# Eight identity products ahead of the feed-forward part's first transpositions, and other settings of the order there and in the start

## The chip, the core and the metric

The kernel runs on one core of a Trainium2 chip. Time is the device time of one execution in microseconds (us). A core has a matrix engine (TensorE, PE in the profile, with its weight loads as PEld), a vector engine (DVE), a scalar engine (ACT), a general engine (POOL) and a sync engine (SP) that here issues nearly all transfers between the main memory and the core. Each engine takes its instructions strictly in the order in which the program lists them, and waits on semaphores where an operand comes from another engine.

## What is computed

One transformer block on 2048 rows of 512 numbers, in 32-bit floats: a conditioned normalization, windowed attention (32 heads of 16, each row sees itself and the 255 rows before it), a second conditioned normalization and a gated feed-forward part of width 1792.

```python
mod = (_silu(c) @ w_mod).reshape(c.shape[0], 6, 1, -1)
sa, ca, ga, sb, cb, gb = (mod[:, i] for i in range(6))
h = _layernorm(x) * (1 + ca) + sa
x = x + ga * _A_ref(h, A_wqkv, A_wo)              # softmax(q k^T / 4, window 256) v, then wo
h = _layernorm(x) * (1 + cb) + sb
x = x + gb * _B_ref(h, B_w1, B_w3, B_w2)          # (silu(h w1) * (h w3)) w2
```

## The kernel before

Matrix products are made from two parts of each operand (a rounded high part and the rest), three products for each full one. The work has four stretches.

**The start.** The rows are loaded in 16 tiles of 128, the six modulation vectors are computed (`modulation`), the rows are normalized, transposed and split (`ln1`, in four blocks of 512 rows; `ring_fill` clears buffers of the scores on POOL), the values of all 16 tiles are computed (`values`, PE line L653), and the first steps of the attention's units are done: `unit_a` (queries and keys, PE L438, with `rows` copying them into place) for three units, `unit_b` (row maxima: a PE product L485 per half, a maximum on DVE L494 each, then `parts` on DVE, `turn` on PE L509, `cut` on ACT and `rows` on SP) for two. Everything here has a key: `W` gives the times of the groups, `Y` the offsets inside `unit_a` and `unit_b`. The list sorted by these keys is the order of the program, and with it that of each engine.

**The units.** 32 units of attention follow (8 groups of four heads times 4 blocks of 512 rows). Step u runs `unit_a` for one unit, `unit_b` for one that is further and `unit_c` for u itself (scores L753, masks by DVE or POOL, exponentials on ACT, products with the values L721), by the keys in `X`, which the change leaves alone.

**The change-over.** Units whose key is at or above TS = 229.9 go into a second list, `fixed`, at times from the map `us` (constants `TW`), and a planner (`Sched.deal`) deals all remaining operations of the program between and behind them: the denominators of the attention (`o_sums`: a load, a reciprocal on DVE L1072, a store), their products with the outputs and the split into two parts (`o_part`: loads L1087 and L1092, DVE or POOL L1104, ACT L1096, DVE or POOL L1099), the output projection (`o_proj`, PE L1116) with the sums of the second normalization behind it (`add_stats`, DVE L985, ACT L993), that normalization (`ln_rstd`, `ln2`: ACT L1236, transpositions on PE L1250, ACT L1254, sums on DVE or POOL L1267, parts L1273 and L1275), and the loads and splits of weights (`load_w`, `load_w2`: SP L1174 and L1217, ACT L967, POOL L968). The planner starts an operation at the earliest time at which its operands are there by its own estimates; among those that are ready on an engine the lowest key wins. Keys come from `K`. Three constants widen the estimates: `RATE` and `QUIET` (transfers), `PEM` (added to the time at which an operand from ACT, DVE or POOL is there for PE) and `DM` (added to the time at which a transfer is there for an engine that uses it, for operations before the end of the `fixed` list). `K["by"][b][k]` names the engines of `o_part` (product, difference); `K["be"]` those of the splits in `load_b`.

**The feed-forward part.** Two halves of 1024 rows, seven pairs of column blocks each: products L1378 (`ffn`), gate and up combined on ACT, DVE and POOL, products L1471 with the second weight, sums into the rows, stores. Its order is dealt by the same planner.

Of the kernel before, what the change touches and what calls it, by code (L numbers as in the profile page):

```python
# [18 lines left out]
P = 128  # L19
# [20 lines left out]
         10.575, 10.975, 11.087, 6.249, 6.261), o=(11.83, 12.324), job=(0.275, 3.004, 9.681), gate=7.93)  # L40
Y = dict(wqk=(-1.668, 4.008, 4.272), pj=(0.205, 0.587, 0.969, 1.18, 1.719, 2.115, 2.497, 2.879, 3.261,
         3.583, 3.954, 4.423), ev=(4.619, 4.869), mix=(5.37,), row=(4.926, 4.905, 4.873, 5.915, 5.14, 5.105,
         6.405, 6.405, 6.405), mx=(0.022, 0.523, 1.023, 1.523, 2.023, 2.822, 3.023, 3.33, 4.051, 4.523, 5.023,
         5.249, 6.023, 6.523, 7.023, 7.523), tl=(0.092, 0.371, 0.331, 0.34, 0.405, 0.331, 0.331, 0.331, 0.331,
         0.331, 0.331, 0.331, 0.331, 0.119, 0.331, 0.331), mr=(8.465, 8.547, 8.884, 10.016))
MODE = 'CDCPCDCP'
W = dict(m=0.18, s=0.307, a=0.29, t=0.562, p=0.366, vs=1.748, vo=0.433, wq=(-1.444, 1.47, 1.587), wv0=-2.239, wvh=(-0.578, -0.445, -0.399, -0.345), wvl=(-0.193, -0.326, -0.374, -0.317), wp=1, A0=2.112, h0=0.452, h=6.002, hb=6.868, ls=3.035, la=0.875, rf=(-1.1, -0.393, 6.445), v=2, vt=1.562, mr=(-1.837, 1.507), mm=(3.653, 5.841, 7.356, 7.655), ml=(-1.346, 1.651, 2.536, 6.904), A=1.465, At=7.897, B=10.563)
MXB = 3
STB = 3
MODL = 'CECECECE'  # L50
NL = 3
XB = 6
PTB = 9
# [202 lines left out]
INF = float("inf")  # L256
RATE = 320.0

QUIET = 1.487
KEY = 1.715  # L260
# [3 lines left out]
def us(t):  # L264
# [3 lines left out]

TW = (231.0, 241.0, 0.8, 0.583)

# [19 lines left out]

@with_exitstack
def block_kernel(ctx: ExitStack, tc: tile.TileContext, x, wqk, wv, wo, w13, w2, c, wmod, out):
    nc = tc.nc
# [4 lines left out]
    ident = cst.tile([P, P], F32, name="ident")  # L298
# [87 lines left out]
    for hh in range(2):  # L386
        m = mskq[HP * hh:HP * hh + HP]
# [213 lines left out]
    wvh = p0.tile([P, KC, D], F32R, name="wvh")  # L601
    wvl = p0.tile([P, KC, D], F32R, name="wvl")
# [69 lines left out]
    h0 = -40.0  # L672
# [17 lines left out]
    for b in range(1, NB):  # L690
        h = h0 + W["h"] + W["hb"] * (b - 1)
# [532 lines left out]
    def ln2(half, key):  # L1224
# [17 lines left out]
        def rows_k(k, key):  # L1242
            h = {}
            for n, (kk, t) in enumerate(((k, 0), (k + 2, 1), (k, 1), (k + 2, 0))):
                bk = Bank("up")
                hk, hn = (half, k, kk, t), f"t{n}"

                def turn(kk=kk, t=t, bk=bk):
                    for i in range(4):
                        nc.tensor.transpose(ps(bk)[:, i * P:(i + 1) * P],  # L1250
                                            tiles["xn", half, 4 * t + i][:, kk * P:(kk + 1) * P], ident)
# [354 lines left out]
```

## Time and profile before

| | us |
|---|---|
| median of three runs | 954.08 (952.42 to 954.97) |
| the profiled execution, its own time | 952.06 |
| its span, from the first instruction to the last | 950.3 |
| PE busy in it | 916.3 |
| DVE, ACT, POOL busy | 670.0, 525.1, 545.6 |

Everything below is read from one execution. Its time is 1.76 us more than its span, which lies outside the first and the last instruction, and 2.02 us under the median. A row of the timeline has the start, the length, the engine, the line, the operation with output and input, the count, and in brackets for how long the engine had been idle and what ended that. A row of the windows has, for each engine, the busy time in a stretch and the number of instructions, then the mean clock that PE was granted (1.00 is full), the busy share of the transfer engines and their GB/s.

### The profile page before, as it was taken

To read this page: it belongs to the slowest core of one execution; us is meant where nothing else is said; L and a number is where in the kernel's file an instruction comes from. 1 tells how busy PE (TensorE), PEld (TensorE's weight loads), DVE (VectorE), ACT (ScalarE), POOL (GpSimd) and SP (SyncE) were. 2 spreads that over 40 slices of the span, in tenths; PEclk is the share of its full clock that TensorE was granted. 3 is DMA by queue.
4 is the path that set the end of the run, shared out by engine and by line. 5 is a ranking of instruction groups with operands and counts; after the bars stand their busy time and mean duration, and the time that the engine had idled before them with its cause. 6 is when DMAs were issued, how large, how long until landed. Compare 5 with 4: busy or idle time off the path is not lost.

```text
span 950.3 us, 16719 instructions
## 1 busy us (share of the span) xinstructions
PE 916.3 (96%) x5330; PEld 710.3 (75%) x5330; DVE 670.0 (71%) x1861; ACT 525.1 (55%) x1031; POOL 545.6 (57%) x694
## 2 busy tenths in 40 slices
PE   5999999999999999988987999999999999999998
PEld 3688677777777777755765878888888888888886
DVE  7675789888898989876668565665558645566465
ACT  3333777777777777766577754333455334433330
POOL 6220566676757566645566789977659546453420
PEclk9999899999999999988989999999999999999999
DMA  8621465555655555565960659645244512323002
GB/s 296 200 80 46 113 185 163 158 146 164 183 156 150 170 157 147 136 183 167 298 220 12 221 199 322 222 171 166 90 161 157 187 41 99 99 62 97 26 23 89
DMA packets 125020, 141.62 MB, mean 149 GB/s; under 512 B 60034, under 2 KB 72834, under 8 KB 124932
## 3 DMA queue, kind: packets, MB, share of 16 engines
q1 hardware_dynamic: 124212, 139.51, 48.0%
q10 hardware_dynamic: 720, 1.05, 0.3%
q8 instruction: 42, 0.69, 0.3%
q14 instruction: 46, 0.38, 0.1%
HBM read 85.72 MB, written 34.61 MB: 127 GB/s over the span
## 4 chain that ended last, share of the span: by engine, by line
PE 78%; DVE 6%; DMA 4%; POOL 4%; ACT 3%; issue 2%; SPq 2%; POOLq 0%; DVEq 0%; ACTq 0%
PE st L1378 11%; PE mx L1378 10%; PE pj L438 8%; PE st L753 8%; PE mx L485 8%; PE po L721 8%; PE st L1471 7%; PE mx L1471 7%; PE st L653 5%; PE pj L1378 3%; PE pj L1471 2%; DMA r_dr<-mT 1%; DVE t L1267 1%; DVE b L1275 1%; DMA qk<-o_dr 1%
## 5 line engine op out<-in xcount | busy, mean ns | idle before, releaser
L494 DVE CUSTOM_DVE_ANT_0 junk<-mx,mskq 128x320 bf16<-128x320 f32 (+4 forms) x512 | 223.4, 464 | 39.6 <-PE mx L485 39.0
L968 POOL TENSOR_TENSOR w<-w,w 128x512 fp32r<-128x512 f32 (+2 forms) x56 | 107.0, 1924 | 111.6 <-ACT w L967 61.8
L485 PE MATMUL mx<-ringk,ringq 96*128 96x320 f32 (+4 forms) x512 | 154.9, 326 | 2.2 <-DVE mt L494 2.2
L753 PE MATMUL st<-ringq,ringk 98*128 98x256 f32 (+1 forms) x528 | 141.9, 338 | 6.8 <-DVE st L773 2.5
L780 POOL TENSOR_SCALAR_AFFINE_SELECT pt<-pt 128x256 f32<-128x256 f32 x224 | 92.4, 413 | 74.7 <-ACT pt L768 67.0
L438 PE MATMUL pj<-hT,wq 128*128 128x512 f32 x384 | 132.5, 403 | 0.3 <-DVE wq L427 0.3
L485 PEld LDWEIGHTS mx<-ringk,ringq 96*128 96x128 f32 x512 | 98.6, 193 | 41.4 <-DVE mt L494 23.1
L768 ACT ACTIVATE pt<-st 128x512 f32<-128x512 f32 (+1 forms) x198 | 115.2, 587 | 24.7 <-DVE st L773 10.5
L753 PEld LDWEIGHTS st<-ringq,ringk 98*128 98x128 f32 x528 | 91.8, 194 | 22.2 <-ACT pt L768 5.8
L721 PE MATMUL po<-pt,vS 128*17 128x384 f32 (+2 forms) x1408 | 92.7, 394 | 0.0
L438 PEld LDWEIGHTS pj<-hT,wq 128*128 128x128 f32 x384 | 68.4, 192 | 7.8 <-DVE wq L427 0.8
L1378 PE MATMUL st<-b,w 128*128 128x512 f32 x270 | 67.8, 391 | 1.3 <-ACT t L1412 1.3
L1409 DVE TENSOR_TENSOR t<-st,t 128x512 f32<-128x512 f32 x48 | 33.0, 688 | 43.3 <-PE st L1378 28.5
L1409 DVE TENSOR_TENSOR t<-mx,t 128x512 f32<-128x512 f32 x49 | 33.5, 687 | 41.8 <-PE mx L1378 28.0
L721 PEld LDWEIGHTS po<-pt,vS 128*17 128x17 f32 x1408 | 34.6, 98 | 36.3 <-issue 19.8
L1449 ACT ACTIVATE wq<-g 128x512 fp32r<-128x512 f32 x28 | 17.7, 631 | 77.2 <-DVE g L1405 38.1
L1378 PE MATMUL mx<-b,w 128*128 128x512 f32 x240 | 59.9, 389 | 0.0
L773 DVE COPY_PREDICATED st<-later,st 128x256 f32<-128x256 uint8 x112 | 47.5, 424 | 17.3 <-PE st L753 12.7
L1378 PEld LDWEIGHTS st<-b,w 128*128 128x128 f32 x270 | 50.5, 188 | 12.1 <-ACT t L1412 1.7
L795 POOL TENSOR_SCALAR_AFFINE_SELECT sm<-sm 128x256 f32<-128x256 f32 x109 | 42.3, 406 | 29.5 <-ACT sm L785 28.6
L761 DVE TENSOR_TENSOR st<-st,mskr 128x256 f32<-128x256 f32 x125 | 53.6, 429 | 8.0 <-PE st L753 8.0
L967 ACT ACTIVATE w<-w 128x512 fp32r<-128x512 f32 (+2 forms) x56 | 42.5, 786 | 20.7 <-DMA w<-wsum 11.2
(256 smaller groups left out, 2010.6 us busy)
## 6 DMA issues: line engine op xcount, KB each, us to landing
ringq<-qk SPq DMA_DIRECT2D x192, 64.0 KB
ringk<-qk SPq DMA_DIRECT2D x96, 128.0 KB
o_dr<-os SPq DMA_DIRECT2D x32, 256.0 KB
w<-wsum SPq DMA_DIRECT2D x14, 512.0 KB
w<-w2g SPq DMA_DIRECT2D x14, 512.0 KB
jb<-in_w SPq DMA_DIRECT2D x24, 256.0 KB
wraw<-in_w SPq DMA_DIRECT2D x7, 768.0 KB
w<-wraw SPq DMA_DIRECT2D x14, 384.0 KB
```

What stands on the lines that cost most here:

```text
L438: nc.tensor.matmul(v["ps"], WQ[g][w][:, n // 3], hTp(i, n // 3, b * BT, BT), start=(n == 0), stop=(n == 3 * KC - 1))
L485: nc.tensor.matmul(v[i][:, :n], both_queries(a, gs), keys(NS, a, (gs + 1) * HP - n, n), start=True, stop=True)
L494: nc.vector.tensor_tensor_reduce(out=junk[:, :n], in0=v[i][:, :n], in1=mskq[:, WK - n:], scale=1.0, scalar=-3e38, op0=ALU.add, op1=ALU.max ...
L721: nc.tensor.matmul(po[32 * i:32 * i + DH + 1, qb * P:(qb + nq) * P], vS[:, kb, 4 * g + i], pts[i // 2][:, i % 2, c0:c0 + nq], start=first, ...
L753: nc.tensor.matmul(o, keys(NM, a, kb * P, P), queries(a, q, n), start=q == lo, stop=not plus and q + n == hi, skip_group_check=True)
L761: nc.vector.tensor_tensor(out=ps, in0=ps, in1=mskk[:, p:p + 1].to_broadcast([P, 2, P]), op=ALU.add)
L768: nc.scalar.activation(held[u, j, a][:, :, :n], v[j, a, 0].rearrange("p (h q) k -> p h q k", h=2)[:, :, :n], AF.Exp, scale=SCALE)
L780: nc.gpsimd.affine_select(out=pt[:, :, 2 * m], in_=pt[:, :, 0], **w)
L968: sch.op(eng, lambda: on_eng(eng).tensor_tensor(out=lo(), in0=src(), in1=hi().bitcast(F32), op=ALU.subtract), 0.06 + 0.0024 * n if eng == ...
L1378: nc.tensor.matmul(ps(bk), WT[s, n][w][:, col], BB[t, k][r], start=start and c == 0, stop=stop and c == 5, skip_group_check=True)
L1409: return nc.vector.tensor_add(o, x, y)
L1471: nc.tensor.matmul(ps(bk), tiles[hk + (h,)][:, i * P:(i + 1) * P], w2_of(last, y, f), start=(m == 0), stop=(m == 5))
```

## The change

Two lines of code are new, and all else is settings.

- `warm` issues `WARM` = 8 products of the 128x128 identity with itself into a bank, each overwriting the last. The first of the `turn` steps of `ln2` (half 0, k = 0, n = 0) calls it on its own bank, ahead of its four transpositions, which then overwrite it too.
- `Y` and `W`: other keys in the start. `ring_fill` for blocks 1 and 2 now sorts ahead of the first normalization on POOL, three of its steps; the load of the first query and key weight sorts behind a modulation load and two row loads on SP; the transposition at the end of `unit_b` and some of its maxima sort later.
- `RATE`, `QUIET`, `TW`, `PEM` and `DM`: other constants of the planner's estimates.
- `K`: other keys in the change-over and in the feed-forward part, and other engines for some operations of `o_part` (23 of 32 on DVE where 19 were) and one of `load_b`.

```diff
-Y = dict(wqk=(-1.668, 4.008, 4.272), pj=(0.205, 0.587, 0.969, 1.18, 1.719, 2.115, 2.497, 2.879, 3.261,
...
-         5.249, 6.023, 6.523, 7.023, 7.523), tl=(0.092, 0.371, 0.331, 0.34, 0.405, 0.331, 0.331, 0.331, 0.331,
-         0.331, 0.331, 0.331, 0.331, 0.119, 0.331, 0.331), mr=(8.465, 8.547, 8.884, 10.016))
+Y = dict(wqk=(-2.274, 2.035, 4.308), pj=(-0.1, 0.569, 1.019, 1.185, 1.631, 2.138, 2.581, 2.993, 3.444,
...
+         5.397, 6.313, 6.725, 7.257, 7.718), tl=(0.539, 1.433, 0.647, 1.142, 0.648, 0.741, 0.109, 0.647, 0.639,
+         0.646, 2.763, 0.647, 0.227, 0.297, 1.447, 0.683), mr=(9.213, 9.684, 10.036, 14.166))
-W = dict(m=0.18, s=0.307, a=0.29, t=0.562, p=0.366, vs=1.748, vo=0.433, wq=(-1.444, 1.47, 1.587), wv0=-2.239, wvh=(-0.578, -0.445, -0.399, -0.345), wvl=(-0.193, -0.326, -0.374, -0.317), wp=1, A0=2.112, h0=0.452, h=6.002, hb=6.868, ls=3.035, la=0.875, rf=(-1.1, -0.393, 6.445), v=2, vt=1.562, mr=(-1.837, 1.507), mm=(3.653, 5.841, 7.356, 7.655), ml=(-1.346, 1.651, 2.536, 6.904), A=1.465, At=7.897, B=10.563)
+W = dict(m=0.106, s=0.303, a=0.131, t=0.578, p=0.595, vs=2.009, vo=0.842, wq=(0.936, 2.347, 2.661), wv0=-3.975, wvh=(-1.912, -0.894, -0.883, -0.579), wvl=(-1.713, 0.802, -0.23, 0.164), wp=1, A0=2.849, h0=0.56, h=6.275, hb=6.499, ls=3.26, la=1.215, rf=(-3.29, -3.105, 2.388), v=1.909, vt=1.543, mr=(-1.923, 1.19), mm=(4.949, 5.639, 7.788, 7.782), ml=(-1.73, 1.363, 1.447, 7.099), A=2.348, At=8.404, B=10.694)
+WARM = 8
-RATE = 320.0
+RATE = 299.475
-QUIET = 1.487
+QUIET = 1.657
-TW = (231.0, 241.0, 0.8, 0.583)
+TW = (231.0, 241.0, 0.8, 0.611)
-PEM = 0.998
-DM = 0.076
+PEM = 1.262
+DM = 3.359
-         ('POOL', 'POOL'), ('DVE', 'POOL')), hr=2.855, de=12.48, wo=-3.567, x1=16.6, xb=-38.041, xl=-26.167,
-         os=-0.13, ol=(-17.833, -5.162, -9.509, 10.002), pl=(11.205, -2.398, -4.869, 102.62), pe=(0.914, -2.635,
-         56.103, 231.635), o=(2.337, 8.384, 18.214, 9.324), n=(1, 1, 2, 1), w0=67.715, l2=2.802, f=2.068,
-         fl=40.1, by=((('POOL', 'POOL'), ('DVE', 'DVE'), ('DVE', 'POOL'), ('DVE', 'DVE')), (('DVE', 'DVE'),
-         ('DVE', 'POOL'), ('DVE', 'POOL'), ('DVE', 'DVE')), (('POOL', 'POOL'), ('DVE', 'DVE'), ('DVE', 'POOL'),
-         ('POOL', 'DVE')), (('DVE', 'POOL'), ('DVE', 'POOL'), ('DVE', 'POOL'), ('DVE', 'POOL'))), w=-2.134,
-         dn=1.412, ds=0.003, l3=-10.82)
+         ('POOL', 'DVE'), ('DVE', 'POOL')), hr=-6.211, de=0.969, wo=-6.368, x1=4.266, xb=-12.052, xl=-14.242,
+         os=2.058, ol=(-15.53, -11.029, -7.444, 0.822), pl=(5.2, -14.242, -17.703, 101.932), pe=(1.564, -3.906,
+         55.497, 233.263), o=(6.308, 9.841, 14.839, 13.354), n=(2, 1, 1, 1), w0=80.926, l2=5.192, f=3.484,
+         fl=37.767, by=((('DVE', 'DVE'), ('DVE', 'DVE'), ('DVE', 'POOL'), ('DVE', 'DVE')), (('POOL', 'DVE'),
+         ('DVE', 'DVE'), ('POOL', 'DVE'), ('POOL', 'POOL')), (('DVE', 'DVE'), ('DVE', 'DVE'), ('DVE', 'DVE'),
+         ('POOL', 'DVE')), (('DVE', 'POOL'), ('DVE', 'POOL'), ('DVE', 'DVE'), ('DVE', 'POOL'))), w=3.067,
+         dn=1.899, ds=0.094, l3=-18.084)
+    def warm(bk, n):
+
+        for _ in range(n):
+            nc.tensor.matmul(bk[:, :P], ident, ident, start=True, stop=True, skip_group_check=True)
...
-                def turn(kk=kk, t=t, bk=bk):
+                def turn(kk=kk, t=t, bk=bk, first=not (half or k or n)):
+                    if first:
+                        warm(ps(bk), WARM)
```

More of the change, by code (lines that the diff above doesn't have):

```diff
@@ L40 @@
          10.575, 10.975, 11.087, 6.249, 6.261), o=(11.83, 12.324), job=(0.275, 3.004, 9.681), gate=7.93)
-Y = dict(wqk=(-1.668, 4.008, 4.272), pj=(0.205, 0.587, 0.969, 1.18, 1.719, 2.115, 2.497, 2.879, 3.261,
-         3.583, 3.954, 4.423), ev=(4.619, 4.869), mix=(5.37,), row=(4.926, 4.905, 4.873, 5.915, 5.14, 5.105,
-         6.405, 6.405, 6.405), mx=(0.022, 0.523, 1.023, 1.523, 2.023, 2.822, 3.023, 3.33, 4.051, 4.523, 5.023,
-         5.249, 6.023, 6.523, 7.023, 7.523), tl=(0.092, 0.371, 0.331, 0.34, 0.405, 0.331, 0.331, 0.331, 0.331,
-         0.331, 0.331, 0.331, 0.331, 0.119, 0.331, 0.331), mr=(8.465, 8.547, 8.884, 10.016))
+Y = dict(wqk=(-2.274, 2.035, 4.308), pj=(-0.1, 0.569, 1.019, 1.185, 1.631, 2.138, 2.581, 2.993, 3.444,
+         3.62, 3.997, 4.395), ev=(4.796, 4.866), mix=(5.178,), row=(5.197, 4.961, 7.863, 6.705, 5.104, 5.164,
+         8.358, 7.097, 7.085), mx=(1.657, 0.757, 0.899, 2.059, 0.694, 2.617, 3.235, 3.564, 4.037, 4.806, 5.263,
+         5.397, 6.313, 6.725, 7.257, 7.718), tl=(0.539, 1.433, 0.647, 1.142, 0.648, 0.741, 0.109, 0.647, 0.639,
+         0.646, 2.763, 0.647, 0.227, 0.297, 1.447, 0.683), mr=(9.213, 9.684, 10.036, 14.166))
 MODE = 'CDCPCDCP'
-W = dict(m=0.18, s=0.307, a=0.29, t=0.562, p=0.366, vs=1.748, vo=0.433, wq=(-1.444, 1.47, 1.587), wv0=-2.239, wvh=(-0.578, -0.445, -0.399, -0.345), wvl=(-0.193, -0.326, -0.374, -0.317), wp=1, A0=2.112, h0=0.452, h=6.002, hb=6.868, ls=3.035, la=0.875, rf=(-1.1, -0.393, 6.445), v=2, vt=1.562, mr=(-1.837, 1.507), mm=(3.653, 5.841, 7.356, 7.655), ml=(-1.346, 1.651, 2.536, 6.904), A=1.465, At=7.897, B=10.563)
+W = dict(m=0.106, s=0.303, a=0.131, t=0.578, p=0.595, vs=2.009, vo=0.842, wq=(0.936, 2.347, 2.661), wv0=-3.975, wvh=(-1.912, -0.894, -0.883, -0.579), wvl=(-1.713, 0.802, -0.23, 0.164), wp=1, A0=2.849, h0=0.56, h=6.275, hb=6.499, ls=3.26, la=1.215, rf=(-3.29, -3.105, 2.388), v=1.909, vt=1.543, mr=(-1.923, 1.19), mm=(4.949, 5.639, 7.788, 7.782), ml=(-1.73, 1.363, 1.447, 7.099), A=2.348, At=8.404, B=10.694)
 MXB = 3
```

## The prediction, as put on record before the run

> **What bounds the kernel now.** I read the page's head and its chain of waits first, then the busy time by stretches, then the order in time around the stretches that lose something.
>
> ```profile
> span 950.3 us, 16719 instructions
> PE 916.3 (96%) x5330; PEld 710.3 (75%) x5330; DVE 670.0 (71%) x1861; ACT 525.1 (55%) x1031; POOL 545.6 (57%) x694
> PEclk9999899999999999988989999999999999999999
> PE 78%; DVE 6%; DMA 4%; POOL 4%; ACT 3%; issue 2%; SPq 2%; POOLq 0%; DVEq 0%; ACTq 0%
> ```
>
> PE is busy for 96% of the span and carries 78% of the chain that ended last, so what counts is where PE waits or runs at a lower clock. The stretches show where (the length, PE's busy time, then at the end the mean clock):
>
> ```profile
> 8.52:20.14 11.62, 10.78 (x56) 6.17 (x56) 10.33 (x17) 6.13 (x12) 7.94 (x7) 0.85 0.94 344
> 20.14:92.01 71.87, 71.52 (x359) 54.38 (x356) 49.18 (x141) 26.42 (x47) 12.74 (x11) 1.00 0.40 117
> 94.94:106.00 11.06, 9.04 (x36) 6.25 (x34) 6.12 (x23) 6.66 (x13) 5.46 (x11) 0.69 0.47 122
> 415.70:460.90 45.20, 39.46 (x289) 24.68 (x288) 28.66 (x87) 26.72 (x58) 20.75 (x34) 0.85 0.71 208
> 460.90:480.40 19.50, 19.48 (x92) 15.70 (x84) 13.16 (x27) 12.10 (x23) 13.07 (x9) 1.00 0.98 306
> 480.40:523.00 42.60, 33.54 (x137) 25.79 (x138) 33.07 (x50) 30.75 (x55) 24.86 (x17) 0.88 0.27 91
> 523.00:560.90 37.90, 36.85 (x173) 29.66 (x172) 21.96 (x29) 27.20 (x46) 31.30 (x28) 1.00 0.60 197
> 560.90:944.00 383.10, 382.55 (x1689) 316.37 (x1688) 227.54 (x316) 149.00 (x234) 222.44 (x164) 1.00 0.39 129
> ```
>
> From 20.14 to 92.01 and from 560.90 to 944.00 PE has no gap to speak of and the full clock: there an order can only lose. Idle time and clock are lost in four places. The start loses 11.62 - 10.78 = 0.84 us idle and 0.15 x 11.62 = 1.7 us of clock. The entry into the units (94.94 to 106.00) loses 2.02 idle and 0.31 x 11.06 = 3.4, but its operations stand under the keys `X`, which stay. The end of the attention (415.70 to 460.90) loses 5.7 idle and 0.15 x 45.2 = 6.8. The change-over (480.40 to 523.00) loses 9.1 and 0.12 x 42.6 = 5.1. The last two, 26.7 us, are what the new constants and keys can work on.
>
> **The end of the attention.** The rows of DVE and PE at the two large gaps, and the clock behind each:
>
> ```profile
> 418.45 0.95 DVE L1072 RECIPROCAL wqr<-wqr 96x128 f32<-96x128 f32 x1 [1.74 <-DMA wqr<-o_dr]
> 419.32 0.40 DVE L773 COPY_PREDICATED st<-later,st 128x256 f32<-128x256 uint8 x1
> 419.78 0.58 PE L753 MATMUL st<-ringq,ringk 98*128 98x256 f32 x1 [2.06 <-DVE st L773]
> 434.89 0.94 DVE L1072 RECIPROCAL mT<-mT 32x128 f32<-32x128 f32 x1 [1.74 <-DMA qkr<-o_dr]
> 436.24 1.46 PE L485 MATMUL mx<-ringk,ringq 96*128 96x320 f32 x3 [1.95 <-DVE mt L494]
> 418.00:426.00 8.00, 6.22 (x39) 4.19 (x39) 5.64 (x22) 3.52 (x8) 3.20 (x8) 0.57 0.84 251
> 434.00:442.00 8.00, 6.05 (x36) 3.48 (x35) 4.77 (x19) 2.74 (x6) 4.68 (x8) 0.59 0.68 208
> ```
>
> DVE stands before a reciprocal of `o_sums` (L1072) until its load has landed, 1.74 us each time; the mask merge (L773, row 419.32) and the maxima behind it come late, and PE waits 2.06 and 1.95 us for them. Right behind each gap the clock falls: (1 - 0.57) x 8 = 3.4 us of full-speed work is lost, then (1 - 0.59) x 8 = 3.3.
>
> `DM` goes from 0.076 to 3.359: the planner takes the landed data to be there 3.28 us later and sorts the reciprocal so much further down among the units' DVE work. 3.28 is more than 1.74, so both waits go; what is then late next is PE itself. The reciprocal comes later, but its result is needed only for products that PE does after the units. Four more of the 32 `o_part` steps on DVE add 4 x 0.69 us (row 489.93 below) to an engine that is busy for 28.66 of these 45.20 us: covered. Gain: 2.06 + 1.95 = 4.0 idle, and between nothing and 6.7 of clock, since at full speed PE may be paced by DVE and ACT. Bounds 0 (the next operation waits instead) and -10.7. I take the middle, **-5.4**: the two gaps and 1.4 of clock, because the next stretch is fed by transfers whose share is already 0.98.
>
> The Trainium skill says (TensorE: Matmul & The Clock Gate, HAM oscillation — how this bites in real kernels) that PE falls to half clock through idle gaps above about 3.4 us. By that rule gaps of 2.06 and 1.95 us would not touch the clock, and taking them away would return 4.0 and no more: a sum of -4.5 instead of -5.9, 949.6 us. The two rows of 8 us disagree: the clock fell to half behind gaps well below the rule's length.
>
> **The change-over and the eight products.** Rows at the first transpositions, at DVE's slow stretch, and a like product:
>
> ```profile
> 469.16 0.41 SPq L1217 DMA_DIRECT2D w<-w2g  x1
> 481.18 7.48 POOL L968 TENSOR_TENSOR w<-w,w 128x512 fp32r<-128x512 f32 x4
> 483.36 0.48 PE L1250 MATMUL mx<-ident,wqr 128*128 128x128 f32 x1 [2.98 <-ACT wqr L1236]
> 485.61:490.10 4.49, 4.49 (x12) 3.52 (x13) 4.46 (x6) 1.87 (x5) 3.05 (x2) 0.51 0.97 345
> 486.36 2.85 DVE L1104 TENSOR_TENSOR wq<-wq,wq 128x512 f32<-128x512 f32 x1
> 489.93 0.69 DVE L1104 TENSOR_TENSOR wq<-wq,wq 128x512 f32<-128x512 f32 x1
> 492.43 0.16 DVE L1010 TENSOR_TENSOR nbB<-nmB,rsB 128x4 f32<-128x4 f32 x1 [1.12 <-POOL rsB L1007]
> 505.66 1.76 PE L1116 MATMUL mx<-wo,o 128*128 128x512 f32 x6 [2.68 <-ACT t L1254]
> 519.24 1.20 PE L1116 MATMUL pj<-wo,o 128*128 128x512 f32 x4 [1.46 <-POOL o L1099]
> 41.11 1.05 PE L583 MATMUL mx<-h,o 128*32 128x512 f32 x2
> ```
>
> Eight products of 32-bit operands are added to PE. A product of that type with 512 columns is two instructions, 1.05 us together (row 41.11), so one with 128 columns is about 0.26, eight are **2.1 us**, at half clock 4.2. They need the bank and the identity alone, and stand before transpositions that wait 2.98 us for the normalized rows (row 483.36): the wait hides them at full clock. Without that cover (other work queued ahead) they cost PE 2.1 to 4.2, and all that is queued behind them as much: the four transpositions, then the projection's products (L1116). What they may buy is the clock: 0.49 x 4.49 = 2.2 us in the row 485.61. Little of that reaches the end: behind it PE has work until 505.66 - 2.68 = 503.0 and then waits 2.68 us for the next bank anyway (row 505.66), because DVE is late. So -0.6, from bounds -2.2 and +4.2.
>
> DVE is late here because a product of `o_part` that takes 0.69 us alone (row 489.93) takes 2.85 while POOL splits weights (row 481.18); the second normalization (row 492.43) stands behind it. Of POOL's four splits in that row I take two for the second weight's (it has two in all), whose load is row 469.16. Its key is moved from 74.3, among the four loads of `load_w` (67.7 to 74.7), to 103.4, behind all four (80.9 to 87.9): worked out from `w0`, `dn`, `ds`, `f`, `fl` and the end of the map. That takes two quarters out of the 7.48, and POOL is free later. DVE's surplus over three single products (2 x 0.9 and 2.16, about 4.1 us in all) should fall by some 1.3. And one difference of block 3 goes from POOL to DVE, in the chain that PE waits on for 1.46 us at 519.24: -0.6. The sum for the change-over is -0.6 - 1.3 - 0.6 = **-2.5**; bounds -6.3 (all the 4.1 and the 2.2) and +4.2 (the eight products uncovered, nothing else won).
>
> **The start.** POOL's and DVE's rows at the first normalization, and those at the last row maxima:
>
> ```profile
> 6.65 0.98 POOL L410 MEMSET ringq<- 98x1024 f32 x1
> 10.50 1.03 POOL L330 TENSOR_TENSOR rs0r<-rs0v,nhalf 128x4 f32<-128x4 f32 x1 [2.87 <-DVE rs0v L328]
> 11.47 0.95 POOL L410 MEMSET ringq<- 98x1024 f32 x1
> 12.48 1.11 POOL L412 MEMSET ringk<- 2x1024 f32 x1
> 13.65 2.29 POOL L410 MEMSET ringq<- 98x1024 f32 x2
> 16.00 1.11 POOL L412 MEMSET ringk<- 2x1024 f32 x1
> 11.56 4.66 DVE L340 TENSOR_SCALAR xt<-xt,mv,rs0r 128x512 f32<-128x512 f32 x4 [1.15 <-POOL rs0r L330]
> L340 DVE TENSOR_SCALAR xt<-xt,mv,rs1r x8: 530/542/2041, 28.6 to 72.9; 128x512 f32<-128x512 f32 x8
> 89.75 0.31 PE L485 MATMUL mx<-ringk,ringq 96*128 96x320 f32 x1
> 90.10 0.49 DVE L494 CUSTOM_DVE_ANT_0 junk<-mx,mskq 128x320 bf16<-128x320 f32 x1 [0.36 <-PE mx L485]
> 91.51 0.27 PE L509 MATMUL mx<-ident,mr 128*32 128x128 f32 x1
> ```
>
> By the new `rf`, the clears at 11.47, 12.48, 13.65 (two) and 16.00 sort before the root at 10.50. POOL is free at 7.63, the five need 0.95 + 1.11 + 2.29 + 1.11 = 5.5, and the root starts at 13.1 instead of 10.5: 2.6 late. But the four steps behind it (row 11.56) took 4.66 us beside those clears, and the same step takes 0.54 alone: 4 x 0.54 = 2.2, which is 2.5 less. That cancels: 0, with 1.7 of clock at stake if PE idles longer.
>
> At the end of the start, seven value products stood between the last maximum's product (89.75) and the transposition of the maxima (91.51). By the new keys it is one (26.82, 26.90, then 28.78), and two maxima and two small DVE steps stand in between: 0.31 + 2 x 0.49 and an estimated 2 x 0.2 (as row 492.43) make 1.7 us after the product's start, and PE has 0.4 us of work: +1.3, and the units begin that much later. Another maximum now sorts behind the product that takes over its bank (27.12 against 25.82; three banks rotate): PE waits or not, 0 to 1 in each of two units, I take 0.7 in all. The weight's load that moves on SP is cast on ACT behind steps that wait for PE: nothing, as long as PE still has value products to do first, which the new keys put ahead. The start: **+2.0**, bounds -1 and +5.
>
> **The feed-forward part.** PE is busy for 382.55 of 383.10 us; new keys (`fl`, `dn`, `de`, `w`) reorder work that is there in surplus: 0, bounds ±1.
>
> **The sum.** +2.0 - 5.4 - 2.5 = -5.9. The profiled execution took 952.06 us (span 950.3 and 1.76 around it), so 946.2 for one like it; the median before, 954.08, is 2.0 above, and gives **948.2**.
>
> **The rivals.**
> - *All the clock comes back* (0.26). Both falls of the clock go with their gaps: -10.7 instead of -5.4, 942.9 us. For it: PE had 12.27 of 16 us in those two windows, DVE only 10.41, so DVE isn't full. Against: the next stretch waits for transfers (share 0.98).
> - *The wait moves* (0.17). The attention ends earlier, but the output projection still starts when the last denominators have gone to memory and back, and 0 is left of the 5.4: 953.6 us. For it: the transfer share of 0.98 and 306 GB/s from 460.90 on. Against: PE is busy for 19.48 of 19.50 us there, so its operands lay ready.
> - *The margin starves the projection* (0.11), the slower end. `DM` delays two steps in a row in each block's chain, the reciprocal and the product behind the second load: 2 x 3.28 = 6.6 us. While the projection has operands from earlier blocks, this is covered; once the units end before block 0's and 1's parts are there, PE stands still and everything behind comes 6.6 later: +2.0 + 6.6 - 2.5 = +6.1, 960.2 us. It decides as soon as PE's gap behind the last L721 exceeds the 5.4 won before it. Against: the margin is one of the plan, and an engine that is free runs the step at once.
> - *Short gaps leave the clock alone* (0.04), faster by less: the gaps' 4.0 us come back, the clock's loss has another cause and stays: +2.0 - 4.0 - 2.5 = -4.5, 949.6 us. Only that the clock falls within 2 us of both gaps speaks against it.
>
> **Chances and range.** My forecast has 0.42, with its own range 944 to 951.5. About 0.3%, 2.9 us here, is what can be told from no change. Faster by more: forecast, full clock and short gaps, 0.72; within: the moved wait, 0.17; slower: 0.11. The range leaves out the starved projection and the lowest end of the unknown costs (-10.7 with a start that costs nothing, about 940): 940 to 955.
>
> **What would show it.** *End of the attention:* no DVE idle over 1 us before L1072, and the clock at 1.00 from unit 28 on; the stretch from the first of these loads to the last L721 is 4 to 8 us shorter. *Eight products:* 16 PE instructions of the new line in front of L1250, about 2 us, and the clock above 0.9 behind them; if a transposition follows without any wait, they had no cover. *DVE:* no L1104 above 1.8 us. *Start:* the root at about 13 us, four L340 in under 3 us, and a PE wait of 1 to 2 us before the last L509 of the start. I am wrong if the gaps of PE between 415 and 461 stay at 5 us, or if PE gets a new gap of over 3 us behind the last L721.

## The result and the profile after

The changed kernel took 945.46 us (median of four runs, 943.32 to 948.44) where the kernel before took 953.25 (951.43 to 954.97) in the same comparison: a ratio of 0.9922, 95% interval [0.9893, 0.9952]. In a later comparison (nine runs of it, below as "the changed kernel again") it was 946.16 against 951.02, 0.9948 [0.9929, 0.9968]. The profiled execution shown here is the slowest of the first four, 948.44 us.

The head of its page and the shares of the chain that ended last:

```profile
span 946.6 us, 16713 instructions
PE 914.4 (97%) x5346; PEld 710.1 (75%) x5346; DVE 678.0 (72%) x1866; ACT 525.0 (55%) x1031; POOL 532.5 (56%) x689
PE 78%; DMA 6%; DVE 5%; ACT 5%; POOL 3%; issue 1%; SPq 1%; ACTq 0%; POOLq 0%; DVEq 0%
```

PE carries 78% of the chain, as before. Four stretches; each begins or ends with the same operation as there, or, at 106.00, 415.70 and 523.00, at the same time (length, PE, PEld, DVE, ACT and POOL busy, then clock, transfer share, GB/s):

```profile
8.68:23.65 14.97, 12.89 (x57) 7.67 (x57) 7.46 (x19) 6.65 (x13) 8.87 (x9) 0.77 0.77 277
96.56:106.00 9.44, 7.51 (x35) 5.00 (x34) 5.32 (x22) 6.60 (x12) 5.34 (x11) 0.82 0.41 103
415.70:458.00 42.30, 37.32 (x291) 22.94 (x291) 28.64 (x89) 27.02 (x58) 21.23 (x35) 0.92 0.74 213
479.20:523.00 43.80, 37.78 (x171) 29.24 (x172) 31.56 (x63) 34.83 (x65) 23.17 (x18) 1.00 0.44 146
```

The end of the attention has shrunk by 2.9 us (by 4.0 between two operations that are the same, below) and its clock has risen from 0.85 to 0.92; in the change-over the clock is 1.00 where it was 0.88; and the start is 3.4 us longer at a clock of 0.77. Inside the end of the attention, DVE's and PE's rows with their waits, and then the clock in steps of 10 us:

```profile
425.05 0.94 DVE L1078 RECIPROCAL wqr<-wqr 96x128 f32<-96x128 f32 x1
430.08 0.47 PE L759 MATMUL st<-ringq,ringk 98*128 98x256 f32 x2 [1.51 <-DMA ringq<-mT]
432.63 0.63 PE L491 MATMUL mx<-ringk,ringq 96*128 96x320 f32 x1 [0.71 <-DVE mt L500]
```

```profile
410.00:420.00 10.00, 9.12 (x69) 5.92 (x68) 9.40 (x41) 7.82 (x20) 4.62 (x10) 1.00 0.39 108
420.00:430.00 10.00, 8.34 (x75) 4.98 (x73) 7.43 (x30) 6.80 (x15) 5.77 (x11) 1.00 0.90 270
430.00:440.00 10.00, 9.21 (x53) 6.51 (x53) 6.52 (x24) 5.07 (x10) 4.94 (x9) 0.66 0.76 227
```

The first reciprocal (now L1078) starts without any wait, and the gap of PE at 420 is gone: the clock stays at 1.00 from 410 to 430. But there is still one gap, at 430, in two parts of 1.51 and 0.71 us, and it has another cause: the scores wait for a transfer of the rows of maxima (`ringq<-mT`), in a stretch in which the transfer engines are 90% busy. The second part has a reciprocal before it all the same: it starts at 431.29, without a wait, and holds DVE for 0.94 us ahead of the maximum that PE needs. Behind the gap the clock is 0.66 for ten microseconds. In this execution one of two falls of the clock has gone, and one has stayed.

The change-over, PE's and DVE's rows and POOL's weight splits:

```profile
477.23 1.95 PE L312 MATMUL mx<-ident 128*128 128x128 f32 x16
480.24 0.33 PE L1258 MATMUL mx<-ident,wqr 128*128 128x128 f32 x1 [1.07 <-ACT wqr L1242]
502.82 3.33 PE L1122 MATMUL mx<-wo,o 128*128 128x512 f32 x12 [1.40 <-ACT t L1262]
477.57 1.77 DVE L1016 TENSOR_TENSOR nbB<-nmB,rsB 128x4 f32<-128x4 f32 x1
483.69 1.78 DVE L1110 TENSOR_TENSOR qk<-qk,qk 128x512 f32<-128x512 f32 x1
490.03 0.16 DVE L1016 TENSOR_TENSOR nbB<-nmB,rsB 128x4 f32<-128x4 f32 x1 [1.13 <-POOL rsB L1013]
483.61 3.02 POOL L974 TENSOR_TENSOR w<-w,w 128x512 fp32r<-128x512 f32 x2 [0.74 <-ACT w L973]
```

The eight products (L312) are 16 instructions in 1.95 us. The first transposition behind them still waits 1.07 us, so they were covered, and takes 0.33 where it took 0.48. No product of `o_part` on DVE is above 1.78 us here, beside two splits on POOL (3.02) where there were four (7.48), and PE's wait for the bank behind them is 1.40 instead of 2.68. The two splits that are left are the second weight's (128x512 each); the two that have gone are the first weight's (128x768 and 128x1024) and now run ahead of the transpositions or beside them.

Behind the change-over there is a new gap: at 547.77 PE waits 2.43 us for DVE, where in the kernel before its longest wait for DVE between 523.00 and 560.90 was 0.24, and its longest for any engine 0.60. PE idles 37.90 - 35.35 = 2.6 us in this stretch instead of 1.1, and the clock is 0.95 instead of 1.00.

The start, POOL, DVE, ACT and PE:

```profile
12.60 1.02 POOL L336 TENSOR_TENSOR rs0r<-rs0v,nhalf 128x4 f32<-128x4 f32 x1
13.66 1.92 DVE L346 TENSOR_SCALAR xt<-xt,mv,rs0r 128x512 f32<-128x512 f32 x4 [3.04 <-POOL rs0r L336]
14.60 0.63 ACT L615 ACTIVATE wvh<-vS 128x512 fp32r<-128x512 f32 x1 [8.73 <-DMA vS<-in_wv]
15.65 3.36 PE L592 MATMUL mx<-o,h 128*128 128x1 f32 x16 [2.02 <-ACT h L584]
23.65 0.50 PE L659 MATMUL st<-wvh,hT 128*128 128x512 f32 x1
```

The root runs at 12.60 and the four steps behind it take 1.92 us in place of 4.66, as worked out. What is new: ACT's cast of the value weight (L615) now stands in front of the activation that feeds the modulation (L584), and waits until 14.60 for its load. PE's modulation products wait 2.02 us for it and take 3.36 us (1.95 in experiment 4, without that wait), and the first value product comes at 23.65 instead of 20.14.

### The profile page after: what moved, and what is told of

Read it like the earlier page. It is cut to its first block, busy times and chain, and to the rows that moved or that the text cites. A ratio compares the mean times of both kernels' runs of the same rounds, so it can differ in the third digit from the quotient of the medians.

```text
span 946.6 us, 16713 instructions
## 1 busy us (share of the span) xinstructions
PE 914.4 (97%) x5346; PEld 710.1 (75%) x5346; DVE 678.0 (72%) x1866; ACT 525.0 (55%) x1031; POOL 532.5 (56%) x689
## 4 chain that ended last, share of the span: by engine, by line
PE 78%; DMA 6%; DVE 5%; ACT 5%; POOL 3%; issue 1%; SPq 1%; ACTq 0%; POOLq 0%; DVEq 0%
PE st L1386 11%; PE mx L1386 11%; PE pj L444 8%; PE st L759 8%; PE po L727 8%; PE mx L491 8%; PE mx L1479 6%; PE st L1479 6%; PE st L659 4%; PE pj L1386 3%; PE pj L1479 3%; DVE g L1413 1%; DMA qkr<-o_dr 1%; PE st L637 1%; DMA wq<-r_dr 1%
## 5 line engine op out<-in xcount | busy, mean ns | idle before, releaser
L491 PE MATMUL mx<-ringk,ringq 96*128 96x320 f32 (+4 forms) x512 | 152.9, 323 | 1.0 <-DVE mt L500 0.9
L974 POOL TENSOR_TENSOR w<-w,w 128x512 fp32r<-128x512 f32 (+2 forms) x56 | 98.7, 1778 | 56.6 <-ACT w L973 56.6
L1429 POOL TENSOR_TENSOR t<-t,t 128x512 f32<-128x512 f32 x28 | 37.6, 1342 | 53.0 <-DVE t L1417 53.0
L457 POOL TENSOR_TENSOR qk<-qkr,qk 128x512 fp32r<-128x512 f32 x32 | 41.3, 1291 | 37.8 <-ACT qk L453 37.8
```

The source lines that it names most:

```text
L491: nc.tensor.matmul(v[i][:, :n], both_queries(a, gs), keys(NS, a, (gs + 1) * HP - n, n), start=True, stop=True)
L974: sch.op(eng, lambda: on_eng(eng).tensor_tensor(out=lo(), in0=src(), in1=hi().bitcast(F32), op=ALU.subtract), 0.06 + 0.0024 * n if eng == ...
```

## The experiments

**My theory** was that of the prediction: the gain is the margin `DM`, which takes the reciprocals out of the way of the units' masks and maxima on DVE; the eight products and the start bring nothing or cost a little. **The rivals:** the products and the clock that they hold up carry the gain; the new keys of the change-over do; or the gain lies in the later steps behind transfers, not in the reciprocals. The 12 runs were made in three comparisons of four kernels each; the kernel before had a median of 951.99, 950.79 and 951.02 us in them.

**1. Without the products.**

```diff
-WARM = 8
+WARM = 0
```

> The changed kernel without the eight products (WARM = 0), all else as in it. In the changed kernel's trace the products fill 1.95 us of a wait, the transpositions behind them take 0.33 us each and the 24 projection products 5.60 us, 0.23 each, at full clock. My theory (they keep the clock, but DVE sets what comes next): the clock falls to half behind 480 us, the 24 products take 1.5 to 3 us longer, and the end comes 0 to 1 us later: 945.5 to 946.5. Rival (PE sets the end here): the whole 2.2 to 3.4 us show, 947.7 to 949. Third (the fall of the clock is a matter of the window's phase): no change of the clock at all, 945.5.

Measured: 944.83 us (943.04 to 947.42), 0.9932 [0.9914, 0.9949]. The windows behind the place where the products had been:

```profile
474.00:480.00 6.00, 3.86 (x16) 2.52 (x16) 5.08 (x12) 5.13 (x8) 6.00 (x4) 0.93 0.89 271
480.00:486.00 6.00, 6.00 (x23) 4.80 (x23) 4.40 (x9) 4.54 (x11) 2.94 (x3) 0.79 0.61 198
```

The products do what a reader would hope in their place: without them the clock is 0.93 and 0.79 here, 0.4 + 1.3 = 1.7 us lost, where the changed kernel has 1.00. Over the 8 us from the first transposition on, the clock is 0.57 to 0.79 in all six kernels here that issue no products, and 1.00 in seven of the eight that do (0.79 in the changed kernel with the old margin). But the end does not move.

**2. The products alone, and three times as many.**

```diff
 # the kernel before, with `warm` and its call
+WARM = 8
 # the changed kernel
-WARM = 8
+WARM = 24
```

> The kernel before with the eight products alone. There the first transposition waits 2.98 us, and the clock is 0.51 in the 4.49 us behind it. My theory: the products fit into the wait (about 2 us), the clock stays near 1.00 behind them, the 21 projection products take 4.8 to 5.2 us instead of 7.12, but DVE holds the next step: the end 0 to 0.7 us earlier, 951.3 to 952 with 952 for before. Rival (PE sets the end): the whole 2.2 us, 949.5 to 950. Third (no cover): 954.

Measured: 950.84 us (948.40 to 953.24), 1.0000 [0.9986, 1.0013].

> The changed kernel with 24 products in place of eight. Sixteen instructions took 1.95 us, so 48 take 5.9; the wait they stand in is 1.95 + 1.07 = 3.0 us long. The first transposition thus starts some 2.8 us later, and the projection behind it too. My theory (DVE and ACT set what comes next, PE has slack there): the end 0 to 1.5 us later than the changed kernel, 944.5 to 946.5 with 952 for before. Rival (PE sets the end from here on): the whole 2.8 us, 947 to 948.5.

Measured: 944.58 us (943.05 to 945.86), 0.9937 [0.9917, 0.9957]. With 24 products PE's rows read:

```profile
474.47 5.52 PE L312 MATMUL mx<-ident 128*128 128x128 f32 x48
479.83 0.27 PE L1258 MATMUL mx<-ident,wqr 128*128 128x128 f32 x1
498.50 3.35 PE L1122 MATMUL mx<-wo,o 128*128 128x512 f32 x12 [0.70 <-ACT t L1262]
```

Here the products fill the whole wait: the transpositions follow at once, and the wait for the next bank is 0.70 instead of 1.40. The time is again the same. Eight products, 24 or none: no difference that these runs can show.

**3. The start alone, and the change without the start.**

```diff
 # the kernel before
-Y = dict(wqk=(-1.668, ...
-W = dict(m=0.18, ...
+Y = dict(wqk=(-2.274, ...
+W = dict(m=0.106, ...
 # the changed kernel: the same lines the other way round
```

> The kernel before with the new keys of the start alone (old planner constants and K, no products). My theory (the gain lies in the change-over, the start loses): 1 to 2 us slower than before, 954 to 955.5. Rival (a good part of the gain lies in the start or at the entry): 947 to 951.

Measured: 951.52 us (948.99 to 954.86), 1.0003 [0.9987, 1.0019].

> The changed kernel with the old keys of the start (Y and W of the kernel before), new planner, with the products. In the changed kernel's trace the first value product comes at 23.65 us instead of 20.14, and the first scores at 96.56 instead of 94.36. My theory (the new start costs what its anchor shows at the first scores): the first value product back at 20.1, the first scores at 94.4, the end 2 us earlier than the changed kernel, 943 to 944. Rival (the new start pays at the entry into the units, where the clock fell to half before and did not after): the clock falls again behind 96 us, and the end is 0 to 1.5 us later than the changed kernel, 945.5 to 947.

Measured: 944.70 us (942.50 to 948.80), 0.9934 [0.9909, 0.9959]. The start neither costs nor brings anything that can be measured; my expectations, a cost of 1 to 2 us in the one and 2 us back in the other, both missed.

**4. The casts of the value weight back in their places.**

```diff
-wvh=(-1.912, -0.894, -0.883, -0.579), wvl=(-1.713, 0.802, -0.23, 0.164)
+wvh=(-0.578, -0.445, -0.399, -0.345), wvl=(-0.193, -0.326, -0.374, -0.317)
```

> The changed kernel with eight keys of the start set back: the casts and remainders of the value weight (wvh, wvl), so that the two evictions of the modulation on ACT no longer stand behind a cast that waits for its load until 14.60 us. My theory (that wait is what made the new start late; the earlier clears on POOL gain): first value product at 20 to 21 us instead of 23.65, the end 2 to 3.5 us earlier than the changed kernel, 942 to 943.5. Rival (the later start is covered by the entry's waits): first value product earlier, the end as in the changed kernel, 945 to 946.

Measured: 942.95 us (941.61 to 946.45), 0.9919 [0.9899, 0.9939]. In its start the activations come first and the casts behind them (ACT), and PE has no wait:

```profile
12.46 0.66 ACT L584 ACTIVATE h<-mx 128x256 f32<-128x256 f32 x2 [6.68 <-PE mx L578]
14.66 2.19 ACT L615 ACTIVATE wvh<-vS 128x512 fp32r<-128x512 f32 x4
14.01 1.95 PE L592 MATMUL mx<-o,h 128*128 128x1 f32 x16
19.15 0.50 PE L659 MATMUL st<-wvh,hT 128*128 128x512 f32 x1
```

The first value product comes 4.5 us earlier than in the changed kernel.

**5. The margin alone, and the change without the margin.**

```diff
 # the kernel before
-DM = 0.076
+DM = 3.359
 # the changed kernel: the other way round
```

> The kernel before with DM = 3.359 alone; the planner deals its whole list anew with it. Between the product with the values near 400 us and the last one the kernel before takes 60.3 us, the changed kernel 56.3. My theory (the margin takes the two reciprocals out of the way of the units): that stretch 56 to 57.5 us, no wait of over 1 us on DVE before a reciprocal L1072, and the end 2 to 4 us earlier than before, 948 to 950 with 952 for before. Rival (the keys K and the other constants make the gain): the stretch 59 to 61 and the end as before, 951 to 953. Third (the margin starves the projection when the keys are not made for it): the stretch shorter, but a gap of PE of over 3 us behind the last product with the values, and the end at 954 or later.

Measured: 945.53 us (942.41 to 950.06), 0.9943 [0.9924, 0.9962]. One constant brings nearly the whole gain, more than the 2 to 4 us that I expected.

> The changed kernel with DM = 0.076 again, all else as in it. My theory: the stretch from the product near 400 us to the last one goes back from 56.3 to 59 to 61, waits for loads before the reciprocals come back, and the end comes 2.5 to 4 us later than the changed kernel: 947.5 to 949.5 with 952 for before. Rival (the keys K carry the gain): the stretch stays at 56 to 57, the end at 944 to 946.

Measured: 949.87 us (945.11 to 953.09), 0.9990 [0.9973, 1.0007]. Without it the rest of the change is worth nothing that can be measured. The rows show the old picture back in the changed kernel, DVE's wait, PE's gap and the fall of the clock behind it:

```profile
419.65 0.95 DVE L1078 RECIPROCAL wqr<-wqr 96x128 f32<-96x128 f32 x1 [1.78 <-DMA wqr<-o_dr]
420.98 0.38 PE L759 MATMUL st<-ringq,ringk 98*128 98x256 f32 x1 [2.10 <-DVE st L779]
```

```profile
420.00:430.00 10.00, 8.79 (x48) 6.10 (x49) 7.01 (x30) 6.16 (x14) 5.52 (x10) 0.66 0.70 220
```

**6. Which steps need the margin.** `DM` holds for every step behind a transfer. Two kernels split it.

```diff
-else DM if late(o, u, s) else 0.0
+else (3.359 if getattr(u, "rec", 0) else 0.076) if late(o, u, s) else 0.0   # margin for the reciprocals
+else (0.076 if getattr(u, "rec", 0) else 3.359) if late(o, u, s) else 0.0   # the other kernel: for all but them
...
-sch.op("DVE", lambda: nc.vector.reciprocal(v["lt"][:n], v["lt"][:n]), 0.9, key, [lt], [lt])
+sch.op("DVE", lambda: nc.vector.reciprocal(v["lt"][:n], v["lt"][:n]), 0.9, key, [lt], [lt]).rec = 1
```

> The kernel before, with the margin of 3.359 us given only to the reciprocals of the denominators; every other step behind a transfer keeps 0.076. If the gain comes from the reciprocal that no longer stands in front of the units' masks and maxima on DVE (my theory), this alone gives what the margin gives as a whole: 945 to 947 us, ratio about 0.994, no wait of DVE above 1 us for such a load between 410 and 440, and the PE gap of 2.06 us behind the mask merge gone. If the gain comes from the later steps (products of the outputs with the denominators, casts of weights, and with them PE's order in the projection), it stays at the time of the kernel before, 950 to 951.5.

Measured: 953.19 us (949.12 to 955.73), 1.0019 [1.0005, 1.0034]. My theory falls here: the reciprocals alone bring nothing. DVE, ACT and PE in its profile:

```profile
418.83 0.95 DVE L1072 RECIPROCAL wqr<-wqr 96x128 f32<-96x128 f32 x1 [0.32 <-DMA ringq<-qk]
460.87 0.69 DVE L1104 TENSOR_TENSOR wq<-wq,wq 128x512 f32<-128x512 f32 x1 [2.60 <-DMA wq<-o_dr]
426.16 0.63 ACT L967 ACTIVATE wo<-wo 128x512 fp32r<-128x512 f32 x1 [4.01 <-DMA wo<-wog]
428.48 0.50 PE L753 MATMUL st<-ringq,ringk 98*128 98x512 f32 x1 [1.50 <-ACT pt L768]
481.55 0.47 PE L1250 MATMUL mx<-ident,wqr 128*128 128x128 f32 x1 [3.54 <-ACT wqr L1236]
```

The reciprocal waits 0.32 us, as expected. But now ACT stands 4.01 us before the cast of the projection weight (L967, `wo<-wog`; 1.23 in the kernel before), with exponentials of the units (L768) behind it in its queue, and PE waits 1.50 us for one of them. DVE stands 2.60 us before a product of `o_part`, and the transpositions of the second normalization wait 3.54 instead of 2.98.

> The kernel before, with the margin of 3.359 us given to every step behind a transfer except the reciprocals, which keep 0.076: the mirror of the other. By my theory the DVE wait of 1.74 us and the PE gap of 2.06 us stay, and the time is that of the kernel before, 949.5 to 951.5. By the rival that the gain lies in the later steps it is 945 to 947. If the margin starves the projection, that would show here by itself: slower than 952.

Measured: 957.22 us (954.01 to 959.77), 1.0065 [1.0043, 1.0086]. Its rows of DVE and PE:

```profile
417.92 0.95 DVE L1072 RECIPROCAL wqr<-wqr 96x128 f32<-96x128 f32 x1 [1.73 <-DMA wqr<-o_dr]
419.24 0.39 PE L753 MATMUL st<-ringq,ringk 98*128 98x256 f32 x1 [2.05 <-DVE st L773]
482.31 0.48 PE L1250 MATMUL mx<-ident,wqr 128*128 128x128 f32 x1 [4.57 <-ACT wqr L1236]
516.36 3.86 PE L1378 MATMUL st<-b,w 128*128 128x512 f32 x9 [4.51 <-ACT t L1412]
```

The first reciprocal and PE's gap behind it are as in the kernel before (1.73 and 2.05), no cast on ACT waits in the units, and behind the units PE waits 4.57 and 4.51 us. So each part of the margin alone is a little slower than no margin (1.0019 and 1.0065), and both together are faster. At the end of the attention the rows suggest a reason: the engines take their steps in order, and whichever step is still planned before its data is there stands in front of the units' work, on DVE or on ACT (with the margin alone no cast there waits). Behind the units, where both lose most, the planner deals all steps anew with each kernel; why just these orders come out with the long waits is not settled by these two runs.

**7. The changed kernel again, and the best of the parts together** (casts back, 24 products).

> The changed kernel as it is, for a direct comparison on this chip: 944 to 946, ratio 0.992 to 0.994 by what it showed before. It is also the measure for the start with the casts in their old places: if that wait of a cast costs what the start's rows show, this one is 1.5 to 3 us above the version with the casts back.

Measured: 946.16 us (942.98 to 951.64), 0.9948 [0.9929, 0.9968].

> The changed kernel with the keys of the weight casts as before (the modulation no longer stands behind a cast that waits for its load) and 24 products in place of 8, which covered the wait before the transpositions wholly in the profile. If both hold, 942 to 943.5, some 1.5 to 3 us under the changed kernel as it is and ratio about 0.991; if the 24 products bring nothing to the end, the time with 8 of them and the casts back, 942.95 in its own comparison; if the start's gain is used up by a later wait, the same as the changed kernel, 944 to 946.

Measured: 943.50 us (941.36 to 948.22), 0.9927 [0.9902, 0.9951]. It is 2.7 us below the changed kernel in the same comparison, as the start's rows say, but the two intervals overlap. With the 942.95 of experiment 4 it is the second version with the casts back that lies below the changed kernel as it is here, though the ratio of experiment 4, 0.9919, is that of the changed kernel in its first comparison, 0.9922: a gain is likely and not shown. The further 16 products add nothing to it.

**The parts by stretches.** Two operations are the same in all these kernels: the 24 products with values that start near 400, and the last product with values. Times in us, one profiled execution each:

| kernel | start of the products near 400 | from there to the end of the last one | from there to the end of the span |
|---|---|---|---|
| before | 399.32 | 61.78 | 489.2 |
| products alone | 398.83 | 62.98 | 487.4 |
| start alone | 397.77 | 62.09 | 487.6 |
| changed, old margin | 400.47 | 61.37 | 485.9 |
| margin for the reciprocals | 398.33 | 60.40 | 493.8 |
| margin for the rest | 398.80 | 61.03 | 494.6 |
| margin alone | 401.61 | 57.36 | 489.0 |
| changed | 400.30 | 57.80 | 488.5 |
| changed, again | 399.90 | 56.59 | 487.6 |
| changed, no products | 400.14 | 57.07 | 484.0 |
| changed, 24 products | 398.95 | 56.40 | 485.8 |
| changed, old start | 399.62 | 57.95 | 486.3 |
| changed, casts back | 397.55 | 58.48 | 485.3 |
| changed, casts back, 24 | 396.43 | 56.87 | 486.7 |

The middle column falls into two groups: 61.37 to 62.98 with the old margin (mean 62.1) and 56.40 to 58.48 with the new one (mean 57.3). With the margin the stretch is 4.7 us shorter, whatever else is changed, and with the margin for a part of the steps 1.7 and 1.0. Not all of it is won: some products of the output projection have moved behind the last product with values. Of the kernel before and the changed one, the run of projection products behind it:

```profile
461.83 6.99 PE L1116 MATMUL mx<-wo,o 128*128 128x512 f32 x30
458.83 8.35 PE L1122 MATMUL mx<-wo,o 128*128 128x512 f32 x36
```

Ahead of it stand 15 such products in the kernel before and 9 in the changed one (12 with the margin alone), and one takes 8.35 / 36 = 0.23 us: six are 1.4 us of the 4.0 here, and in the mean of the two groups (14.3 against 9.4) 1.1 of the 4.7. In the last column the four kernels with the old `K` and one margin for all steps have 488.3 in the mean, the eight with the new `K` 486.3, with single ones from 484.0 to 489.2; the two with half a margin have 493.8 and 494.6, and there they lose.

What the 4.7 us are made of, in that stretch of the kernel before, of the changed kernel, and of the changed kernel again:

```profile
399.32:461.10 61.78, 55.93 (x426) 35.83 (x425) 43.78 (x149) 39.61 (x88) 30.78 (x54) 0.89 0.63 185
```

```profile
400.30:458.10 57.80, 52.72 (x420) 33.76 (x419) 42.68 (x147) 39.01 (x85) 30.57 (x53) 0.94 0.65 188
```

```profile
399.90:456.49 56.59, 52.16 (x420) 32.50 (x419) 42.25 (x148) 38.80 (x85) 29.41 (x53) 0.97 0.64 192
```

PE was idle for 61.78 - 55.93 = 5.9 us, and is for 5.1 and 4.4. The clock took 0.11 x 61.78 = 6.8 us, and takes 3.5 and 1.7. So idle time gives 0.8 to 1.4 us. The clock's figures cannot simply be added to it, since they count a low clock while PE stands idle too: 1.4 + 5.1 would be more than the 5.2 us by which the last of the three is shorter. PE's busy time falls by 3.2 and 3.8 us; less the 1.4 that has moved, 1.8 and 2.4 are an estimate of what the clock gives. For the four kernels with the old margin against the eight with the new one, the 4.7 us are 1.5 of idle time, 1.1 of moved work and about 2.1 of clock. The clock of the stretch itself keeps the two groups apart: 0.89, 0.89, 0.92 and 0.92 with the old margin, 0.94 in five and 0.97 in three with the new one.

## Why the prediction was right, and where its steps were not

The forecast of 948.2 us, 5.9 below a run like the profiled one, is met: the medians are 945.46 and 946.16, 7.8 and 4.9 us under those of the kernel before beside them. Its main term is borne out by the runs: the margin alone brings 5.3 us (945.53 against 950.79), where 5.4 were forecast. That the whole sum fits is partly luck: the +2.0 for the start and the -2.5 for the change-over cancel nearly, and the runs show neither clearly. And one of the prediction's own signs of being wrong has come: PE's gaps between 415 and 461 are still 46.00 - 41.02 = 5.0 us in the profile shown (5.7 before). By its own steps:

- **The end of the attention, -5.4: right in size (5.3 in the times; 4.7 in the table, of which 1.1 has only moved), wrong in its parts.** I took the two gaps to go as a whole, 4.0 us, and a fifth of the clock's loss with them, 1.4. The first gap went; the second was closed on DVE and opened again behind a transfer (1.51 and 0.71 us). Idle time gave only 0.8 to 1.4 of the 4.0, and the clock, sized at 1.4, some 1.8 to 2.4: in this stretch more of the gain is clock than idle time.
- **Why the margin works: half right.** That DVE's wait before the reciprocal makes the gap is shown by the changed kernel with the old margin. That the reciprocal is all there is to it is refuted: with the margin for the reciprocals alone the time was 953.19. The rows point to the casts on ACT behind a load as another part (4.01 us before L967 there, no wait with the margin alone); no run gives the margin to them alone, and the prediction did not look at ACT's waits there.
- **The eight products, -0.6: cost right, worth 0.** 1.95 us against an estimate of 2.1, covered by the wait. The clock behind them was won (1.7 us), but nothing of it shows in the time. That it is given back at the wait for the next bank, as the step supposed, is not what the rows say: this wait is 1.13 us without products, 1.40 with eight and 0.70 with 24. Where it goes is open.
- **The change-over, -2.5: DVE came as said but not by the step named, and the size is in doubt.** The load of the second weight is not later (468.41 against 469.16), and its two splits still run beside DVE's products (row 483.61); what has left that row is the first weight's splits. PE's wait of 1.46 us for a difference on POOL fell to 0.16, as worked out. The stretch from the last product with values to the end is 2.0 us shorter in the mean of the profiles; in the times the change without margin is 0.9990 [0.9973, 1.0007], which allows anything from nothing to a gain of 2.6 us for the start, the products and the change-over together.
- **The start, +2.0: mis-sized.** The root and the four steps came as worked out. The wait of 1.3 us before the transposition of the maxima did not come: in the program's order twelve projections of the next unit stand around it, which the keys of the one list did not show. In their place stood a step that I had put at nothing, the casts of the value weight ahead of the modulation, which delays the first value product by 3.5 us here (1.7 in the changed kernel again, 21.82). At the first scores 2.0 of them are left (96.56 against 94.58; 1.0 in the mean of six profiles with the new start against six with the old), near 400 about 1 in this execution and 0.2 in the mean of six against six (399.59 against 399.42); the start alone measures 1.0003. What ate the delay on the way is probably the clock at the entry into the units, 0.82 here and 0.69 before; no run tests it, and it differs from run to run.
- **The feed-forward part, 0:** from 560.90 on PE is still without a gap to speak of. Ahead of that the prediction missed a cost: the wait of 2.4 us for DVE near 545 stands in all seven kernels that have both the new `K` and the new margin, and is under 1 us with either alone.

Of the rivals, *all the clock comes back* was the nearest: in the execution of the changed kernel again 1.7 us of 6.8 were still lost. But some of the clock is lost in all eight profiles with the new margin, and PE's idle time is still 4.0 to 5.9 us in them (5.9 to 6.7 with the old margin). *The wait moves* and *the margin starves the projection* resemble what the two parts of the margin showed (953.19 and 957.22, with the long waits behind the units), but not the change as it is. *Short gaps leave the clock alone* does not fit the two groups of clocks above: behind a gap of 2.10 us (row 420.98 of the changed kernel with the old margin) the clock is 0.66, and in the changed kernel, without that gap, 1.00 over the same ten microseconds. The gap is not all there is to it, as the last section shows. The rule of the Trainium skill that stood behind this rival (TensorE: Matmul & The Clock Gate, HAM oscillation — how this bites in real kernels), gaps above about 3.4 us, does not describe what these runs show.

## What to carry to other kernels

Where engines take their steps in a written order, a step behind a transfer that is planned too early holds up everything behind it on its engine; here a margin paid when all such steps had it (0.9943) and cost a little when only some had it (1.0019 and 1.0065). A gap of PE can cost clock as well as its length, so a step that closes a gap can be worth more than the idle time that the profile shows. Filling a wait with products that nothing needs kept the clock up and was worth nothing at the end: a clock that is won in one place is not yet time. And where a shorter stretch is read as a gain, count the work in it first, since a planner may have moved some of it out.

## What the hardware showed that was not expected

The clock does not follow the length of the last gap alone. With the margin alone, PE's only waits around 420 are these, none above 0.81 us, and the clock falls all the same (a row of 24 products takes 2.76 us there and 1.49 at full clock):

```profile
419.48 0.39 PE L753 MATMUL st<-ringq,ringk 98*128 98x256 f32 x1 [0.58 <-ACT pt L766]
420.49 0.78 PE L753 MATMUL st<-ringq,ringk 98*128 98x256 f32 x4 [0.20 <-ACT pt L768]
423.47 0.63 PE L485 MATMUL mx<-ringk,ringq 96*128 96x320 f32 x1 [0.81 <-DVE mt L494]
424.46 2.76 PE L721 MATMUL po<-pt,vS 128*17 128x384 f32 x24
```

```profile
420.00:430.00 10.00, 8.93 (x51) 5.31 (x49) 6.64 (x27) 4.96 (x12) 3.22 (x8) 0.66 0.81 242
```

In the changed kernel again the clock is 0.83 from 420.00 to 430.00, with waits of 0.58 and 0.21 us before it.

And one and the same gap does both. PE waits 2.42 and 2.45 us for the same operation on DVE in the changed kernel with 24 products and in the changed kernel again; the wait and the window around it:

```profile
543.43 1.66 PE L1386 MATMUL st<-b,wo 128*128 128x512 f32 x6 [2.42 <-DVE t L1417]
540.00:550.00 10.00, 7.58 (x38) 5.91 (x37) 5.45 (x6) 6.70 (x11) 6.08 (x9) 1.00 0.24 91
```

```profile
545.33 1.71 PE L1386 MATMUL st<-b,wo 128*128 128x512 f32 x6 [2.45 <-DVE t L1417]
540.00:550.00 10.00, 7.47 (x27) 5.51 (x27) 6.66 (x6) 8.04 (x14) 7.71 (x10) 0.84 0.20 79
```

The clock is 1.00 in the one and 0.84 in the other. The longest falls here cost about 3.4 us (0.34 of 10 us), and whether a gap brings one differs between executions. That this is a part of the spread of the nine runs of the changed kernel again, 942.98 to 951.64, is likely and not shown, as one of the nine has a profile. The Trainium skill (TensorE: Matmul & The Clock Gate, Part 1: The HAM clock gate) says that PE's activity is watched in windows of about 3.4 us that run freely and so meet a kernel at another phase each time; these two rows agree with that part of the page.

DVE was slow beside POOL even where it does next to nothing: the operation on 128x4 elements (L1016) took 1.77 us while POOL split weights and 0.16 without (rows 477.57 and 490.03 of the changed kernel).
